# Decoding float64 weights on three engines: sign bits written by GpSimd as 16 bits, rescales on ScalarE, first high-part casts on ScalarE

## The chip, the cores and the metric

The kernel runs on one core of a Trainium2 chip. The metric is the device time of one execution in microseconds (us), and lower is better. Times are medians of several executions; one further execution was recorded by the hardware profiler, and all rows below come from it. Engines are named as the profile names them: PE is TensorE (PEld its weight loads), DVE is VectorE, ACT is ScalarE, POOL is GpSimd, SP is the queue that issues most DMAs.

## The reference

Attention with a local window and a few global keys, followed by a feed-forward layer whose activation is a rational function:

```python
scores = scale * np.matmul(q, k.transpose(0, 1, 3, 2))        # 4 batches, 8 heads, 768 x 64
keep = is_global | is_local                                   # 8 global keys, window of 96
bias = -slopes[:, None, None] * dist[None, :, :]
scores = np.where(keep, scores + bias, -1e9)
a = softmax(scores)                                           # 1e-9 added to the sum
x = np.matmul(a, v)                                           # then (3072 tokens, 512)
h = x @ w_in                                                  # 512 x 2048
P = a0 + a1*h + a2*h**2 + a3*h**3
Q = 1.0 + abs(b0)*abs(h) + abs(b1)*h**2
out = ((P / (Q + 1e-6)) @ w_out).astype(np.float32)           # 2048 x 512
```

`w_in` and `w_out` are float64 arrays. [...]

## The kernel before

**Work and order.** Tokens go in 12 chunks of 256. A chunk has 8 attention units (`u`, a pair of heads for 128 tokens) and 8 feed-forward steps (`f`, 256 of the 2048 hidden columns). The feed-forward runs some 10 to 12 units behind the attention. Each piece of work is given a priority (`PRI`, `PRI_A`), and a list scheduler turns priorities and its own estimates of durations into one fixed order per engine; at run time each engine takes its instructions strictly in that order, waiting on semaphores. So moving one operation to another engine can reorder all engines nearby.

**Weights.** Both matrices are cut into 32 pieces of 128 x 512 values, 512 KB each as float64. `first` and `WSCHED` set the order of the pieces: they are numbered 0 to 31 as they are decoded, and `MODE[n]` says how piece `n` is decoded. `fetch` (L182) issues the DMA into one of six raw buffers (three of a pool "raw", three of a pool shared with later tiles `g`). A raw buffer is free for the next fetch when the last decode operation has read it. In a raw buffer the low and the high word of each value lie side by side, so an operation on one of them steps by 8 bytes.

`decode` builds the value in two parts that are joined bit by bit:
- the scaled high word: on ACT as an absolute value (L213; mode 2), or on POOL with its sign, which the later shift throws out (L211; mode 5);
- the three bits that the shift would lose, from the upper half of the low word, on POOL (L215), written as an integer over the low word;
- the sign bit, put beside those three bits on DVE (L218);
- shift by three and join, on DVE (L220). Its output is the float32 piece, `w_..f`.

**Split.** From the second chunk on, the feed-forward uses each weight as a high part in a reduced float32 format plus a remainder, three matmuls per product. `split_w` makes the high part by a cast (L233, on DVE for the pieces in `HI_V`, otherwise ACT) and the remainder by a subtraction (L234, on DVE for the pieces in `LO_V`, otherwise POOL). The first chunk uses the undivided float32 pieces (L274, L353).

**Names.** `r_2_3` is the raw buffer of piece (1, 2, 3), that is row block 2, column block 3 of `w_in`; `r_9` that of row block 9 of `w_out`; `w_..f` the decoded, `w_..h` the high part. The profile leaves the last number of a name out. `tk`, `s`, `tp` and `o` are the attention's PSUM tiles, which share three buffers; `kF` and `qz` hold transposed keys and queries (L413, L415; POOL copies eight global keys into `kF`, L451); L463 masks the scores and takes their maximum on DVE and so frees `s`. `h`, `fu`, `fa`, `fs` and `q` belong to the activation: ACT reads `h` (L306 to L308), DVE builds the numerator (L313, L314) and the quotient (L327 to L329), POOL adds the denominator (L315), and `acc` collects the output of the second matmul.

Of the kernel before, what the change touches and what calls it, by code (L numbers as in the profile page):

```python
# [11 lines left out]
I32 = mybir.dt.int32  # L12
BF16 = mybir.dt.bfloat16
U16 = mybir.dt.uint16
AF = mybir.ActivationFunctionType
ALU = mybir.AluOpType
PSUM = bass.MemoryType.PSUM
# [22 lines left out]

SPLITS = {4: 0, 5: 2, 6: 4, 7: 8, 8: 12, 9: 16, 10: 19, 11: 22, 12: 25, 13: 28, 14: 32}

MODE = (5, 2, 2, 5, 2, 5, 2, 5, 2, 5, 2, 5, 2, 2, 5, 2, 2, 5, 2, 2, 5, 2, 2, 2, 2, 2, 2, 2, 2, 2, 2, 2)
HI_V = (0, 2, 4, 6, 8, 10, 12, 14, 16, 18, 20, 22, 24, 26, 28, 30)
LO_V = (13, 15, 17, 19, 21, 23, 25, 27, 29, 31)


# [58 lines left out]
def tile_kernel(ctx: ExitStack, tc: tile.TileContext, q, k, v, n_global, n_local,  # L106
                w_in, w_out, ca, cb, out):
    nc = tc.nc
# [52 lines left out]
    def piece(dt, key):  # L161
        return wide.tile([P, 2 * TOK], dt, tag="w", name=f"w{'_'.join(map(str, key))}{'f' if dt is F32 else 'h'}",
                         bufs=NCT * DF // (2 * TOK) + NFT + 1)
# [20 lines left out]
    def decode(key):  # L184
# [3 lines left out]
        raw = fetched.pop(key)  # L188
        bits = dst.bitcast(I32)
        top, low = raw.bitcast(I32)[:, :, 1], raw.bitcast(I32)[:, :, 0]  # L190
        half = raw.bitcast(U16).rearrange("p f (w z) -> p f w z", z=2)[:, :, 0, 1]
        mode = MODE[len(full) - 1]
        if mode < 2:


            nc.scalar.activation(out=dst, in_=raw[:, :, 1], func=AF.Abs)
            guard = nc.gpsimd if mode else nc.vector
            guard.tensor_scalar(out=dst, in0=dst, scalar1=1.125 * 2.0 ** -15, scalar2=None, op0=ALU.max)
            nc.vector.tensor_scalar(out=bits, in0=bits, scalar1=3, scalar2=0x3FFFFFFF,
                                    op0=ALU.logical_shift_left, op1=ALU.bitwise_and)  # L200
            nc.vector.scalar_tensor_tensor(out=bits, in0=top, scalar=-0x40000000, in1=bits,
                                           op0=ALU.bitwise_and, op1=ALU.bitwise_or)
            nc.vector.scalar_tensor_tensor(out=bits, in0=low, scalar=29, in1=bits,
                                           op0=ALU.logical_shift_right, op1=ALU.bitwise_or)
# [7 lines left out]
        else:  # L212
            nc.scalar.activation(out=dst, in_=raw[:, :, 1], func=AF.Abs, scale=2.0 ** -112)  # L213
        if mode != 3:
            nc.gpsimd.tensor_scalar(out=low, in0=half, scalar1=2.0 ** -13, scalar2=FLOOR, op0=ALU.mult, op1=ALU.add)  # L215
        else:
            nc.scalar.activation(out=low, in_=half, func=AF.Copy, scale=2.0 ** -13, bias=FLOOR)
        nc.vector.scalar_tensor_tensor(out=low, in0=top, scalar=-0x80000000, in1=low,  # L218
                                       op0=ALU.bitwise_and, op1=ALU.bitwise_or)
        nc.vector.scalar_tensor_tensor(out=bits, in0=bits, scalar=3, in1=low,  # L220
                                       op0=ALU.logical_shift_left, op1=ALU.bitwise_or)

# [8 lines left out]
    def split_w(key):  # L231
        hi[key] = piece(FR, key)
        (nc.vector.tensor_copy if len(hi) - 1 in HI_V else nc.scalar.copy)(out=hi[key], in_=full[key])  # L233
        (nc.vector if len(hi) - 1 in LO_V else nc.gpsimd).tensor_tensor(  # L234
# [14 lines left out]
    def load_coef():  # L249
# [6 lines left out]
        m, y, z, k = (rt[:, x:x + 1] for x in range(4))  # L256
        nc.scalar.activation(out=m, in_=coef[:, 5:6], func=AF.Abs)
        nc.vector.tensor_scalar(out=y, in0=m, scalar1=1e-36, scalar2=None, op0=ALU.max)
        nc.scalar.activation(out=y, in_=y, func=AF.Ln)
        nc.scalar.activation(out=y, in_=y, func=AF.Exp, scale=0.5)  # L260
        nc.vector.reciprocal(out=z, in_=y)
# [298 lines left out]
    def windowed(lates):  # L560
# [37 lines left out]
        for t in range(NU + LAG + F2 + 1):  # L598
# [76 lines left out]
            for n, (kind, j) in enumerate(WSCHED.get(t, ())):  # L675
                tc.cur_priority = base + 1000 * t + pri[False]["dec"] + 50 * n
                for key in pieces(kind, j):
                    decode(key)
# [162 lines left out]
```

## Time and profile before

| | |
|---|---|
| median of 3 runs | 761.07 us (759.77 to 762.39) |
| the profiled execution | 761.35 us |
| its span, first to last instruction | 759.6 us |
| mean granted TensorE clock | 0.991 |
| PE busy | 733.3 us (97%), 5074 matmuls |
| DVE busy | 607.3 us (80%) |
| ACT busy | 578.1 us (76%) |
| POOL busy | 454.8 us (60%) |
| HBM read, written | 35.92 MB, 6.29 MB |

The profiled execution's time is 1.75 us more than its span. The busy shares are means over the whole run. The decoding lies in the first 91 us, in which the weights are also read; the split follows up to 159 us; after that no work on weights is left.

### The profile page before, as it was taken

How to read it: one execution, taken by the hardware profiler on the slowest of the kernel's cores; microseconds unless marked ns; L12 is line 12 of the kernel's file. 1: busy time of each engine (PE TensorE's matmuls, PEld its weight loads, DVE VectorE, ACT ScalarE, POOL GpSimd, SP SyncE). 2: the span in 40 equal slices, each digit the busy share in tenths (PEclk: the TensorE clock that was granted, in tenths of full speed). 3: DMA queues.
4: the chain of work that ended last, by engine and by line, in shares of the span. 5: the costliest groups of instructions: out<-in, count | busy, mean ns of one | idle time of the engine just before them, and what ended most of it. 6: DMA issues, size and time to landing. Idle time of an engine off the chain costs nothing.

```text
span 759.6 us, 15075 instructions
## 1 busy us (share of the span) xinstructions
PE 733.3 (97%) x5074; PEld 637.2 (84%) x5074; DVE 607.3 (80%) x1441; ACT 578.1 (76%) x1301; POOL 454.8 (60%) x490
## 2 busy tenths in 40 slices
PE   5798899999999999999999999999999999999996
PEld 4575566888989999999999989988989988998994
DVE  6899966877798878888788878878888788876564
ACT  5788667976987877877877877877887878876764
POOL 6786564674566765756665656566467566655441
PEclk9999899999999999999999999999999999999998
DMA  8887100114333322323322322233322321200000
GB/s 255 290 272 240 41 22 22 50 25 108 95 78 74 100 62 64 98 62 73 101 54 57 105 60 63 86 76 77 95 53 64 95 68 37 71 16 1 28 1 33
DMA packets 111675, 62.16 MB, mean 82 GB/s; under 512 B 81380, under 2 KB 99812, under 8 KB 111588
## 3 DMA queue, kind: packets, MB, share of 16 engines
q1 hardware_dynamic: 110528, 60.85, 29.5%
q8 instruction: 42, 0.69, 0.4%
q10 hardware_dynamic: 1060, 0.26, 0.2%
q14 instruction: 45, 0.37, 0.2%
HBM read 35.92 MB, written 6.29 MB: 56 GB/s over the span
## 4 chain that ended last, share of the span: by engine, by line
PE 88%; DVE 7%; issue 2%; ACT 1%; DMA 1%; POOL 0%; SPq 0%; DVEq 0%; ACTq 0%
PE h L282 34%; PE acc L358 33%; PE o L524 5%; PE tp L499 5%; PE s L449 5%; PE acc L353 3%; DVE r L218 2%; PE tk L394 1%; PE h L274 1%; PE s L444 1%; DMA r<-in_moe_w_in_dram 1%; DVE pr L463 1%; ACT pr L473 0%; PE o L515 0%; DVE w_3f L220 0%
## 5 line engine op out<-in xcount | busy, mean ns | idle before, releaser
L489 POOL TENSOR_SCALAR pr<-pr,stats 128x256 f32<-128x256 f32 (+1 forms) x152 | 132.0, 879 | 112.3 <-DVE stats L480 65.0
L282 PE MATMUL h<-xh,win_l 128*128 128x256 f32 x704 | 197.4, 281 | 0.0
L315 POOL TENSOR_TENSOR fa<-fa,fs 128x512 f32<-128x512 f32 x95 | 122.9, 1293 | 86.6 <-ACT fs L308 79.6
L358 PE MATMUL acc<-wout_l,g 128*128 128x512 f32 x352 | 139.4, 396 | 0.0
L282 PEld LDWEIGHTS h<-xh,win_l 128*128 128x128 f32 x704 | 133.1, 189 | 1.6 <-issue 0.2
L338 POOL TENSOR_TENSOR g<-fu,g 128x512 fp32r<-128x512 f32 x87 | 113.2, 1301 | 32.6 <-ACT g L337 26.4
L473 ACT ACTIVATE pr<-pr,stats 128x256 f32<-128x256 f32 (+1 forms) x192 | 92.7, 485 | 30.8 <-DVE stats L463 29.9
L306 ACT ACTIVATE fu<-h,coef 128x512 f32<-128x512 f32 (+1 forms) x97 | 75.0, 774 | 30.4 <-PE h L282 24.1
L327 DVE SCALAR_TENSOR_TENSOR fu<-fu,coef,q 128x512 f32<-128x512 f32 (+1 forms) x97 | 71.8, 740 | 27.4 <-ACT q L323 24.1
L322 ACT ACTIVATE fs<-fa,coef 128x512 f32<-128x512 f32 (+1 forms) x97 | 69.5, 716 | 26.0 <-POOL fa L315 24.3
L313 DVE TENSOR_TENSOR fu<-fu,h 128x512 f32<-128x512 f32 (+1 forms) x97 | 65.6, 676 | 20.4 <-ACT fs L308 20.3
L358 PEld LDWEIGHTS acc<-wout_l,g 128*128 128x128 f32 x352 | 66.4, 189 | 9.5
L314 DVE SCALAR_TENSOR_TENSOR fu<-fu,coef,h 128x512 f32<-128x512 f32 (+1 forms) x97 | 71.7, 739 | 1.9
L427 DVE SCALAR_TENSOR_TENSOR kq<-tk,kq 64x256 fp32r<-64x256 f32 x144 | 60.8, 423 | 15.0 <-ACT kq L426 10.7
L501 DVE COPY pT<-tp 128x512 f32<-128x512 f32 (+1 forms) x75 | 48.5, 646 | 30.1 <-PE tp L499 29.0
L328 DVE SCALAR_TENSOR_TENSOR q<-fa,coef,q 128x512 f32<-128x512 f32 (+1 forms) x97 | 72.1, 744 | 0.0
L426 ACT ACTIVATE kq<-tk 64x256 fp32r<-64x256 f32 x144 | 54.2, 376 | 19.7 <-DVE kq L427 12.5
L329 DVE SCALAR_TENSOR_TENSOR fu<-q,fu 128x512 f32<-128x512 f32 (+1 forms) x97 | 66.2, 683 | 1.6
L308 ACT ACTIVATE fs<-h,coef 128x512 f32<-128x512 f32 (+1 forms) x97 | 66.3, 683 | 1.4 <-DMA out_dram<-o 1.2
L337 ACT CAST g<-fu 128x512 fp32r<-128x512 f32 (+1 forms) x89 | 54.8, 615 | 14.7 <-DVE fu L329 14.3
L307 ACT ACTIVATE fa<-h,coef 128x512 f32<-128x512 f32 (+1 forms) x97 | 65.5, 676 | 0.1
L499 PE MATMUL tp<-ident,pr 128*128 128x128 f32 x352 | 58.3, 279 | 4.9 <-ACT kF L415 3.2
(256 smaller groups left out, 2055.8 us busy)
## 6 DMA issues: line engine op xcount, KB each, us to landing
mv<-nat SPq DMA_DIRECT2D x36, 256.0 KB
qT<-kq SPq DMA_DIRECT2D x144, 64.0 KB
r<-in_moe_w_in_dram SPq DMA_DIRECT2D x16, 512.0 KB
r<-in_moe_w_out_dram SPq DMA_DIRECT2D x16, 512.0 KB
nat<-in_q_dram SPq DMA_DIRECT2D x48, 128.0 KB
vt<-in_v_dram SPq DMA_DIRECT2D x48, 128.0 KB
out_dram<-o SPq DMA_DIRECT2D x24, 256.0 KB
nat<-in_k_dram SPq DMA_DIRECT2D x46, 128.0 KB
```

Of the source, the lines that this page charges most:

```text
L282: nc.tensor.matmul(out=hps[f][:, y, :], lhsT=w[:, fs], rhs=x[:, ct, :], start=(n == 0), stop=(n == 3 * NCT - 1))
L306: nc.scalar.activation(out=u, in_=h, func=AF.Identity, scale=a3, bias=a2)
L314: nc.vector.scalar_tensor_tensor(out=u, in0=u, scalar=a1, in1=h, op0=ALU.add, op1=ALU.mult)
L315: side(f).tensor_tensor(out=a, in0=a, in1=s, op=ALU.add)
L322: nc.scalar.activation(out=s, in_=a, func=AF.Ln, bias=q1)
L327: nc.vector.scalar_tensor_tensor(out=u, in0=u, scalar=a0, in1=r, op0=ALU.add, op1=ALU.mult)
L328: nc.vector.scalar_tensor_tensor(out=r, in0=a, scalar=q1, in1=r, op0=ALU.add, op1=ALU.mult)
L338: side(f).tensor_tensor(out=g[:, 1, ys], in0=u, in1=g[:, 0, ys], op=ALU.subtract)
L358: nc.tensor.matmul(out=acc, lhsT=gs[f][:, z, y, ts], rhs=w, start=(ft == 0 and n == 0), stop=(ft == NFT - 1 and n == 2))
L473: nc.scalar.activation(out=d, in_=d, func=AF.Exp, scale=-1.0, bias=st[:, x:x + 1], accum_out=st[:, 2 + 2 * x:3 + 2 * x])
L489: nc.gpsimd.tensor_scalar(out=d, in0=d, scalar1=st[:, 6 + x:7 + x], scalar2=None, op0=ALU.mult)
L499: nc.tensor.transpose(out=t_ps[:, x, w, :], in_=pr[:, x, w, :], identity=ident)
```

## The change

`MODE` gets a new value, 6, for the 14 odd pieces from 3 to 29. In mode 6 ACT makes the scaled absolute value, POOL makes the three bits as before, and POOL then writes the sign as a 16-bit integer, 0 or -32768, into the upper half of the word that holds the three bits. DVE's L218 is left out for these pieces and only the shift and join remains. Eight of the nine pieces that were in mode 5 leave it (six for mode 6, two for mode 2); piece 0 keeps it. `HI_V` changes too: the casts of pieces 0, 2, 4, 6, 8 and of all later even ones go to ACT, and those of the odd pieces from 9 to 31 go to DVE.

```diff
+I16 = mybir.dt.int16
...
-MODE = (5, 2, 2, 5, 2, 5, 2, 5, 2, 5, 2, 5, 2, 2, 5, 2, 2, 5, 2, 2, 5, 2, 2, 2, 2, 2, 2, 2, 2, 2, 2, 2)
-HI_V = (0, 2, 4, 6, 8, 10, 12, 14, 16, 18, 20, 22, 24, 26, 28, 30)
+MODE = (5, 2, 2, 6, 2, 6, 2, 6, 2, 6, 2, 6, 2, 6, 2, 6, 2, 6, 2, 6, 2, 6, 2, 6, 2, 6, 2, 6, 2, 6, 2, 2)
+HI_V = (9, 11, 13, 15, 17, 19, 21, 23, 25, 27, 29, 31)
 LO_V = (13, 15, 17, 19, 21, 23, 25, 27, 29, 31)
...
-        nc.vector.scalar_tensor_tensor(out=low, in0=top, scalar=-0x80000000, in1=low,
-                                       op0=ALU.bitwise_and, op1=ALU.bitwise_or)
+        if mode == 6:
+            sign = raw.bitcast(I16).rearrange("p f (w z) -> p f w z", z=2)[:, :, 0, 1]
+            nc.gpsimd.tensor_scalar(out=sign, in0=raw[:, :, 1], scalar1=0.0, scalar2=-32768.0,
+                                    op0=ALU.is_lt, op1=ALU.mult)
+        else:
+            nc.vector.scalar_tensor_tensor(out=low, in0=top, scalar=-0x80000000, in1=low,
+                                           op0=ALU.bitwise_and, op1=ALU.bitwise_or)
         nc.vector.scalar_tensor_tensor(out=bits, in0=bits, scalar=3, in1=low,
                                        op0=ALU.logical_shift_left, op1=ALU.bitwise_or)
```

In the changed kernel the lines above the new branch stand one further down (L213 is L214, L215 is L216), the sign is L221, the old L218 is L224, the old L220 is L226, and everything below stands six further down.

What each engine is given, in order, differs up to the third chunk and is the same after it. Three places follow. First POOL, at the pieces 19 to 28, before; the numbers behind a name tell one buffer use from another:

```order
L211 TENSOR_SCALAR w_8f<-r_8_761 128x512
L215 TENSOR_SCALAR r_8_761<-r_8_761 128x512
L215 TENSOR_SCALAR r_9_768<-r_9_768 128x512
L215 TENSOR_SCALAR r_0_3_775<-r_0_3_775 128x512
L451 COPY kF<-kGF 128x8
L215 TENSOR_SCALAR r_1_3_782<-r_1_3_782 128x512
L215 TENSOR_SCALAR r_2_3_860<-r_2_3_860 128x512
L215 TENSOR_SCALAR r_3_3_867<-r_3_3_867 128x512
L315 TENSOR_TENSOR fa_736<-fa_736,fs_737 128x512
L215 TENSOR_SCALAR r_10_931<-r_10_931 128x512
```

POOL now, from the same three bits of piece 22 on:

```order
L216 TENSOR_SCALAR r_0_3_775<-r_0_3_775 128x512
L216 TENSOR_SCALAR r_1_3_782<-r_1_3_782 128x512
L221 TENSOR_SCALAR r_9_768<-r_9_768 128x512
L457 COPY kF<-kGF 128x8
L216 TENSOR_SCALAR r_2_3_860<-r_2_3_860 128x512
L221 TENSOR_SCALAR r_1_3_782<-r_1_3_782 128x512
L216 TENSOR_SCALAR r_10_931<-r_10_931 128x512
L216 TENSOR_SCALAR r_3_3_867<-r_3_3_867 128x512
L321 TENSOR_TENSOR fa_736<-fa_736,fs_737 128x512
L216 TENSOR_SCALAR r_12_1016<-r_12_1016 128x512
L221 TENSOR_SCALAR r_3_3_867<-r_3_3_867 128x512
```

A sign stands three or four places behind the three bits of its piece, and a kF copy or a sum for the activation can stand behind a sign. Second DVE, between two groups of L463, before:

```order
L218 SCALAR_TENSOR_TENSOR r_11_938<-r_11_938 128x512
L314 SCALAR_TENSOR_TENSOR fu_735<-fu_735,coef,h_717 128x512
L218 SCALAR_TENSOR_TENSOR r_12_1016<-r_12_1016 128x512
L552 TENSOR_TENSOR o_840<-o_840,rs_854 128x256
L220 SCALAR_TENSOR_TENSOR w_10f<-w_10f,r_10_931 128x512
L233 CAST w_2_0h<-w_2_0f 128x512
L218 SCALAR_TENSOR_TENSOR r_13_1023<-r_13_1023 128x512
L220 SCALAR_TENSOR_TENSOR w_11f<-w_11f,r_11_938 128x512
L327 SCALAR_TENSOR_TENSOR fu_735<-fu_735,coef,q_810 128x512
L328 SCALAR_TENSOR_TENSOR q_810<-fa_736,coef,q_810 128x512
L313 TENSOR_TENSOR fu_817<-fu_817,h_799 128x512
L220 SCALAR_TENSOR_TENSOR w_12f<-w_12f,r_12_1016 128x512
```

DVE now, between the same two groups:

```order
L226 SCALAR_TENSOR_TENSOR w_10f<-w_10f,r_10_931 128x512
L224 SCALAR_TENSOR_TENSOR r_12_1016<-r_12_1016 128x512
L226 SCALAR_TENSOR_TENSOR w_12f<-w_12f,r_12_1016 128x512
L484 TENSOR_REDUCE stats<-stats 128x2
L486 RECIPROCAL stats<-stats 128x2
L333 SCALAR_TENSOR_TENSOR fu_735<-fu_735,coef,q_810 128x512
L334 SCALAR_TENSOR_TENSOR q_810<-fa_736,coef,q_810 128x512
L558 TENSOR_TENSOR o_840<-o_840,rs_854 128x256
L226 SCALAR_TENSOR_TENSOR w_3_3f<-w_3_3f,r_3_3_867 128x512
L335 SCALAR_TENSOR_TENSOR fu_735<-q_810,fu_735 128x512
L224 SCALAR_TENSOR_TENSOR r_14_1093<-r_14_1093 128x512
L319 TENSOR_TENSOR fu_817<-fu_817,h_799 128x512
```

The sign operations of the odd pieces and the cast are gone, and `fu_735` is finished ahead of the second group. Third PE, from the transposes `tp_921` on, before:

```order
L499 MATMUL tp_921<-ident,pr_792 128x128 x4
L353 MATMUL acc_0_747<-w_2f,fu_647 128x512
L353 MATMUL acc_0_747<-w_3f,fu_647 128x512
L353 MATMUL acc_1_757<-w_2f,fu_647 128x512
L353 MATMUL acc_1_757<-w_3f,fu_647 128x512
L444 MATMUL s_944<-kF,qz 128x256 x2
L400 MATMUL tk_960<-ident,nat_557 128x128 x2
L274 MATMUL h_889<-x_277,w_0_2f 128x256
```

PE now, up to the same transposes:

```order
L359 MATMUL acc_1_757<-w_2f,fu_647 128x512
L359 MATMUL acc_1_757<-w_3f,fu_647 128x512
L280 MATMUL h_889<-x_277,w_0_2f 128x256
L280 MATMUL h_889<-x_277,w_1_2f 128x256
L280 MATMUL h_889<-x_277,w_2_2f 128x256
L280 MATMUL h_889<-x_277,w_3_2f 128x256
L280 MATMUL h_889<-x_277,w_0_2f 128x256
L505 MATMUL tp_921<-ident,pr_792 128x128 x4
```

Feed-forward matmuls have moved ahead of the transposes: four `acc` (the other two stand a few rows up) and five `h`. In the same way the four `acc` of `w_4f` and `w_5f` and the eight `h_955` behind them now stand ahead of `o_996`.

## The prediction

> **What bounds the kernel now.** I read the page's slices first, then stretches, the chain, PE's waits and single instructions. The slices hold busy tenths:
>
> ```profile
> PE   5798899999999999999999999999999999999996
> ...
> DVE  6899966877798878888788878878888788876564
> ...
> PEclk9999899999999999999999999999999999999998
> ```
>
> A slice is 19 us. TensorE is full from the sixth slice on, so whatever is gained or lost is decided in the first 100 us. The stretches confirm that (columns: from and to, length, us busy and instructions of PE, PEld, DVE, ACT and POOL, granted clock, DMA share, GB/s):
>
> ```profile
> 10.00:45.00 35.00, 26.68 (x171) 19.62 (x170) 29.73 (x90) 25.70 (x89) 27.27 (x29) 0.95 0.93 293
> 45.00:70.00 25.00, 24.45 (x143) 18.64 (x143) 24.93 (x52) 21.64 (x51) 18.36 (x19) 1.00 0.75 231
> 70.00:100.00 30.00, 25.25 (x106) 16.03 (x102) 29.07 (x58) 21.14 (x49) 18.64 (x19) 0.89 0.27 85
> 100.00:700.00 600.00, 600.00 (x4330) 533.22 (x4329) 485.20 (x1160) 470.40 (x1040) 366.78 (x393) 1.00 0.26 67
> ```
>
> From 100 to 700 us PE has no idle time: a start made earlier by a microsecond ends a microsecond earlier. From 45 to 100 us PE idles 0.55 + 4.75 = 5.3 us, while DVE has 54.0 of 55 us filled, ACT 42.8 and POOL 37.0. The chain that ended last, asked for 9 to 86 us alone, names the engine:
>
> ```profile
> by line: DVE r L218 23.9%; issue 15.4%; DMA r<-in_moe_w_in_dram 8.4%; DVE pr L463 7.0%; ACT pr L473 4.1%; DVE w_3f L220 3.7%; DVE fu L313 3.2%; DVE w_2f L220 3.1%; DVE q L328 2.8%; DVE w_0f L220 2.8%; PE s L444 2.7%; POOL r L215 2.3%; POOL
> ```
>
> L218, the operation that mode 6 drops, has 23.9% of 77 us = 18.4 us of that chain, 0.58 us for each of its 32. What DVE's lateness costs PE is two gaps, and a lower clock behind each (waits of PE; then its instructions in time: start, us):
>
> ```profile
> PE tp L499 <- ACT kF L415: 2.6, 1, 2.6
> PE o L515 <- DVE stats L463: 2.5, 2, 2.1
> ```
> ```profile
> 72.95 1.12 PE L499 MATMUL tp<-ident,pr 128*128 128x128 f32 x4 [2.62 <-ACT kF L415]
> 73.86 1.92 PE L353 MATMUL acc<-w_2f,fu 128*128 128x512 f32 x2
> 75.56 1.44 PE L353 MATMUL acc<-w_3f,fu 128*128 128x512 f32 x2
> 76.84 1.02 PE L353 MATMUL acc<-w_2f,fu 128*128 128x512 f32 x2
> ...
> 83.09 0.60 PE L499 MATMUL tp<-ident,pr 128*128 128x128 f32 x4
> 85.75 0.44 PE L515 MATMUL o<-ident,stats 128*64 128x128 f32 x4 [2.06 <-DVE stats L463]
> ...
> 88.22 1.11 PE L499 MATMUL tp<-ident,pr 128*128 128x128 f32 x4
> 89.13 1.48 PE L353 MATMUL acc<-w_4f,fu 128*128 128x512 f32 x2
> ```
>
> Idle: 2.62 + 2.06 = 4.7 us. After the first gap the same work takes 1.12, 1.92 and 1.44 us instead of 0.60, 1.02 and 1.02 (1.8 us lost), after the second 1.11 and 1.48 instead of 0.60 and 1.02 (1.0 us). Together 7.5 us that a less loaded DVE could give back in this stretch.
>
> **The change part by part.** Prices (mean ns stand behind the busy time; of L211 and L215 minimum/median/maximum):
>
> ```profile
> L218 DVE SCALAR_TENSOR_TENSOR r<-r 128x512 int32<-128x512 int32 x32 | 25.9, 816 | 1.8 <-POOL r L215 1.8
> L215 POOL TENSOR_SCALAR r<-r x32: 641/860/1647, 11.0 to 80.3; 128x512 int32<-128x512 uint16 x32
> L211 POOL TENSOR_SCALAR w_0f<-r x2: 1523/1684/1845, 9.4 to 14.2; 128x512 f32<-128x512 f32 x2
> sum 91.00, POOL 15.63; mean POOL 7.82
> L213 ACT ACTIVATE w_3f<-r 128x512 f32<-128x512 f32 x4 | 2.7, 684 | 0.0
> L233 ACT CAST w_1h<-w_1f 128x512 fp32r<-128x512 f32 x3 | 1.9, 617 | 0.2
> L233 DVE CAST w_0h<-w_0f 128x512 fp32r<-128x512 f32 x2 | 1.3, 645 | 0.0
> L233 DVE CAST w_1h<-w_1f 128x512 fp32r<-128x512 f32 x2 | 0.8, 414 | 0.0
> ```
>
> - (a) Fourteen L218 go from DVE: 14 x 0.82 = 11.4 us of work, on the chain 14 x 0.58 = 8.1 us.
> - (b) Casts: high parts 0, 2, 4, 6, 8 leave DVE, 9 and up in odd numbers replace 10 and up in even ones. Before 100 us DVE loses four (1.3 + 0.8 = 2.1 us) and ACT gains four (4 x 0.62 = 2.5 us). Later DVE makes twelve where it made twelve, with nobody waiting on PE.
> - (c) Eight pieces leave mode 5. GpSimd loses eight of its nine L211 (15.63 / 9 = 1.74 us each, 13.9 us); ScalarE gains eight rescales at 0.68 us, 5.5 us; six of them fall before 45 us.
> - (d) GpSimd gains fourteen sign writes, an operation that the trace does not have: float32 in, a compare and a multiply, 16 bits out, both with gaps of 8 bytes. Nearest rows: L215, two ALU operations and 16 bits on one side, at least 0.64 us; L211, the same float32 input, 1.52 us. I take 1.54 us, by the input. Fourteen cost 21.6 us (9.0 at 0.64), so GpSimd's balance is +7.7 us (-4.9 at the low end). The high end is open: if each ALU operation costs what L211's one does, 3.1 us and 43 us.
>
> GpSimd's cover from 45 to 100 us: 37.0 us filled, less two L211 (3.5), plus eight signs, of pieces 15 to 29 (12.3) = 45.8 of 55 us. It holds, and would be used up at a sign of (55 - 33.5) / 8 = 2.7 us. Behind each sign in its queue wait the kF copies for the scores and the fa sums of the feed-forward, by one sign at most; the decode of an odd piece waits for it on DVE, where the order puts it behind the next even piece.
>
> ACT from 45 to 100 us: 42.8 + 2.5 (casts) + 1.4 (two rescales) = 46.7 of 55 us. Its cover is 12.2 us of idle time, part of it waiting for DVE or PE; I put 1.5 of the added 3.9 us on the path.
>
> The order takes up DVE's relief: tp_921, the first gap, now stands behind four acc and five h matmuls, and o_996, the second, behind acc of w_4f and w_5f. Those need DVE's fu earlier than before, which (a) allows. The transfers follow, since a raw buffer is freed by DVE's last operation on it:
>
> ```profile
> SPq L182 <- DVE w_3f L220: 4.7, 3, 2.8
> ACT w_10f L213 <- DMA r<-in_moe_w_out_dram: 1.1, 1, 1.1
> ```
>
> In odd pieces that release now waits for GpSimd's sign, and on SP the next q and k loads wait behind it. In the changed order they still stand between the weights, several units ahead of their use; I put this at nothing, with 2.8 us (the longest such wait) as its upper end.
>
> Before 45 us the first h waits for the attention of chunk 0:
>
> ```profile
> 44.85 1.03 PE L274 MATMUL h<-x,w_0f 128*128 128x256 f32 x4
> ```
>
> DVE's chain gets shorter by 6 x 0.58 = 3.5 us, ACT busier by 6 x 0.68 = 4.1 us on 25.7 of 35, DMA is 0.93 busy: I take nothing, with -3.5 and +4.1 as ends.
>
> Sum: -7.5 (gaps and clock) + 1.5 (ACT) = -6.0 us. The profiled execution took 761.35 us (span 759.6), 0.28 us above the median of 761.07: 755.4 us.
>
> **A rule against it.** What GpSimd does beside DVE is in the trace (GpSimd's and DVE's instructions in time):
>
> ```profile
> 35.12 1.54 POOL L211 TENSOR_SCALAR w_3f<-r 128x512 f32<-128x512 f32 x1
> 78.89 1.33 POOL L315 TENSOR_TENSOR fa<-fa,fs 128x512 f32<-128x512 f32 x1
> ```
> ```profile
> 35.21 1.72 DVE L218 SCALAR_TENSOR_TENSOR r<-r 128x512 int32<-128x512 int32 x2
> ...
> 79.01 1.76 DVE L218 SCALAR_TENSOR_TENSOR r<-r 128x512 int32<-128x512 int32 x1
> ...
> 84.33 0.68 DVE L218 SCALAR_TENSOR_TENSOR r<-r 128x512 int32<-128x512 int32 x1
> ```
>
> Beside L315, with two inputs, DVE's L218 stood still for most of its length (1.76 us, against 0.68 with GpSimd idle). Beside L211, with one, two L218 took 1.72 us together, some 0.4 us more than twice 0.68. So a one-input sign should hold DVE up by about 0.4 us, not by its 1.54.
>
> The Trainium skill, "SBUF — State Buffer", section "Who interferes with whom", says otherwise: VectorE with two SBUF inputs and a GpSimd operation that reads SBUF exclude each other for the whole instruction. The L315 row agrees, the L211 row does not. By that rule rival 1 below would be the outcome.
>
> **Rivals.**
> 1. *The relief is taken back by the shared access or by ACT: no change.* Were exclusion complete, signs would cost the pair 14 x 1.54 = 21.6 us against 13.9 + 14 x 0.68 = 23.4 us given back: 1.8 us over the whole start, 1 us or so in the end, 760.5. ACT alone could do it too, by 5.5 + 2.5 = 8.0 us of new work. The L211 row speaks against the first, ACT's idle time against the second. 25%.
> 2. *GpSimd becomes the bound: slower.* From a sign of 2.7 us on. At 3.1 us it has 33.5 + 8 x 3.1 = 58.3 us to do in 55, +3.3 us, and before that 27.3 - 6 x 1.74 + 6 x 3.1 = 35.5 in 35, +0.5 us: 765.2. For it: a float32 tensor_scalar costs 1.52 us with one ALU operation. Against: L215 has two at 0.64 us. 20%.
> 3. *All of the chain comes back.* 8.1 + 0.9 (the cast at 78 us) = 9.0 us, with a sign near L215's price and an earlier first h: 752.4. 10%.
>
> **How the numbers follow.** The forecast (755.4, own range 753 to 759) has 45%. About 0.3%, 2.3 us, is what a measurement of this kernel can tell from no change (its three runs lay 2.6 us apart): below 758.8 faster, above 763.4 slower. Faster: 0.44 of the forecast's 0.45 and rival 3, 0.54. Same: rival 1 and what is left, 0.27. Slower: 0.19. The range goes from rival 3 to beyond rival 1, to where the start's +4.1 or the q and k loads' +2.8 take part of the forecast's gain and more: 752 to 764. It leaves out most of rival 2.
>
> **What would show it.** Right: signs of 0.6 to 1.9 us; L218 at 18; PE's two gaps gone and the clock near 1.00 from 70 to 100 us; DVE with idle time there; a first h within 3 us of 45. Wrong: signs over 2.7 us, GpSimd full to 90 us with kF and fa late; PE waiting for ACT casts or rescales; or DVE's two-input operations stretched by a sign's length.

## The result, and the profile after

| | before | after |
|---|---|---|
| median of 5 runs | 759.77 us (758.76 to 762.39) | 765.40 us (764.38 to 765.43) |
| ratio of the means, 95% interval | | 1.0064 [1.0044, 1.0085] |
| span of the profiled execution | 759.6 us | 763.6 us |

The change makes the kernel 0.64% slower, some 5 us. 755.4 us were predicted, and 765.4 lies above the range too. The sign's own row, and the row of the three bits behind which it stands (minimum/median/maximum, first and last start):

```profile
L221 POOL TENSOR_SCALAR r<-r x14: 2692/3042/3213, 15.2 to 95.3; 128x512 int16<-128x512 f32 x14
L216 POOL TENSOR_SCALAR r<-r x32: 639/1088/1195, 11.0 to 99.2; 128x512 int32<-128x512 uint16 x32
```

A sign costs 2.69 us where none of DVE's decode or activation operations runs beside it, and 3.04 in the median: twice the 1.54 us that the sum took, and above the 2.7 us at which GpSimd's cover was to end. The page's slices show where it goes:

```profile
PE   5698889999999999999999999999999999999996
...
DVE  6658786879788888888788778788888788886565
...
POOL 6999986575567666656556657565466656665441
PEclk9999999999999999999999999999999999999998
```

DVE's full slices have gone, and POOL has taken their place from the second to the fifth. The stretches:

```profile
10.00:45.00 35.00, 26.32 (x148) 18.94 (x147) 24.42 (x77) 26.79 (x87) 32.81 (x26) 0.95 0.93 286
45.00:70.00 25.00, 22.73 (x133) 17.59 (x133) 17.18 (x45) 19.06 (x47) 23.75 (x19) 1.00 0.66 197
70.00:100.00 30.00, 25.98 (x131) 16.25 (x130) 23.59 (x45) 20.37 (x50) 28.88 (x20) 1.00 0.41 123
```

POOL fills 52.6 of the 55 us from 45 to 100 (before: 37.0), DVE 40.8 (before: 54.0), and PE idles 2.27 + 4.02 = 6.3 us (before: 5.3). DVE and ACT now wait for POOL, and PE for DVE behind them (waits of DVE and of ACT from 9 to 105 us, of PE from 45 to 105 us):

```profile
DVE r L224 <- POOL r L216: 10.8, 13, 1.9
DVE w_5f L226 <- POOL r L221: 2.8, 1, 2.8
```
```profile
ACT fs L328 <- POOL fa L321: 8.7, 4, 4.9
```
```profile
PE acc L359 <- DVE fu L335: 3.2, 2, 2.4
```

One place in time, on POOL, ACT, DVE and PE:

```profile
74.86 3.20 POOL L221 TENSOR_SCALAR r<-r 128x512 int16<-128x512 f32 x1
78.14 2.42 POOL L216 TENSOR_SCALAR r<-r 128x512 int32<-128x512 uint16 x2
80.64 1.81 POOL L321 TENSOR_TENSOR fa<-fa,fs 128x512 f32<-128x512 f32 x1
```
```profile
82.48 0.72 ACT L328 ACTIVATE fs<-fa,coef 128x512 f32<-128x512 f32 x1 [2.28 <-POOL fa L321]
```
```profile
87.69 0.68 DVE L335 SCALAR_TENSOR_TENSOR fu<-q,fu 128x512 f32<-128x512 f32 x1
```
```profile
88.42 1.12 PE L359 MATMUL acc<-w_4f,fu 128*128 128x512 f32 x2 [2.43 <-DVE fu L335]
```

The last input of this `fa` sum was written at 72.74 us (ACT's L314, 72.03 and 0.71 long). The sum starts at 80.64, because the sign of 3.20 us and the three bits of other pieces stand before it in POOL's order. ACT stands still for it; DVE, which has the L224 of a piece ahead of the rest of `fu` in its order, stands still for 1.90 us until 83.23 for the three bits behind the sum; and PE gets its longest gap between 45 and 105 us.

Not every gap is the sign's. The longest before 45 us is 2.29 us, ahead of the scores matmuls at 37.31, and the profile puts it down to POOL's L216. But ACT's copy into `kF`, which they read, ends only at 37.21, and in run 5, where the sign is short, the same matmuls start at 37.47. The eight h matmuls behind them, before and after:

```profile
37.59 1.89 PE L274 MATMUL h<-x,w_0f 128*128 128x256 f32 x8
```
```profile
40.32 2.85 PE L280 MATMUL h<-x,w_0f 128*128 128x256 f32 x8
```

The clock is 1.00 from 37.5 to 39.5 us before and 0.65 from 40.0 to 43.2 in the change. Run 5 has these eight at 39.54 us with 2.65 us, so most of this delay does not come from the length of the sign.

A mark that both kernels pass is the first matmul with split weights, before and after:

```profile
115.08 0.68 PE L282 MATMUL h<-xh,w_0h 128*128 128x256 f32 x1
```
```profile
119.08 0.47 PE L288 MATMUL h<-xh,w_0h 128*128 128x256 f32 x1
```

It is 4.0 us late, and so is the end (763.6 against 759.6). In both, 486 matmuls stand before the mark, and from it to the end it is 644.5 us: all was lost before it. I use it below; a mark comes from one execution, and runs 13 and 14, which turned out as two of the same, have it 1.8 us apart.

### The profile page after: what moved, and what is told of

Read it like the earlier page. It is cut to its first block, busy times and chain, and to the rows that moved or that the text cites. A ratio compares the mean times of both kernels' runs of the same rounds, so it can differ in the third digit from the quotient of the medians.

```text
span 763.6 us, 15062 instructions
## 1 busy us (share of the span) xinstructions
PE 734.6 (96%) x5074; PEld 636.7 (83%) x5074; DVE 596.5 (78%) x1423; ACT 582.9 (76%) x1313; POOL 484.2 (63%) x496
## 4 chain that ended last, share of the span: by engine, by line
PE 87%; POOL 4%; DMA 3%; DVE 2%; issue 2%; ACT 1%; SPq 0%; POOLq 0%; DVEq 0%
PE h L288 33%; PE acc L364 32%; PE o L530 5%; PE tp L505 5%; PE s L455 4%; PE acc L359 2%; POOL r L216 2%; PE tk L400 1%; PE h L280 1%; PE s L450 1%; POOL r L221 1%; DMA r<-in_moe_w_in_dram 1%; DMA vt<-in_v_dram 1%; POOL win_l L240 1%; DMA r<-in_moe_w_out_dram 0%
## 5 line engine op out<-in xcount | busy, mean ns | idle before, releaser
L321 POOL TENSOR_TENSOR fa<-fa,fs 128x512 f32<-128x512 f32 x95 | 124.5, 1311 | 86.5 <-ACT fs L314 81.9
L479 ACT ACTIVATE pr<-pr,stats 128x256 f32<-128x256 f32 (+1 forms) x192 | 92.7, 485 | 27.9 <-DVE stats L469 27.0
L314 ACT ACTIVATE fs<-h,coef 128x512 f32<-128x512 f32 (+1 forms) x97 | 66.3, 683 | 1.2 <-DMA out_dram<-o 0.7
```

The source lines that it names most:

```text
L321: side(f).tensor_tensor(out=a, in0=a, in1=s, op=ALU.add)
L479: nc.scalar.activation(out=d, in_=d, func=AF.Exp, scale=-1.0, bias=st[:, x:x + 1], accum_out=st[:, 2 + 2 * x:3 + 2 * x])
```

## The experiments

G is the theory that what the sign occupies makes the kernel slow (S in the first texts: its time on GpSimd alone). Against it stand A, ScalarE's added work, and O, the order that the list scheduler makes. All ratios are to the kernel before, on the same chip, with 95% intervals. In every kernel made from the changed one the sign keeps its line, L221, but for the two tables of prices.

**1. The sign from 16 bits.**

```diff
-in0=raw[:, :, 1]                    # float32
+in0=words[:, :, 1, 1]               # its upper 16 bits as int16
```

> The sign operation reads the upper 16 bits of the high word as int16 instead of the whole word as float32; the same two ALU operations, the same int16 output, the same function, and every engine has the same instructions in the same order as in the changed kernel. Three theories. S (the price of the sign operation fills GpSimd): the price comes from the float32 input, as in L212's 1.52 us for one ALU operation; with 16-bit input the sign costs 0.64 to 1.2 us as L216 does with two ALU operations, 14 of them give back 20 to 28 us of GpSimd between 15 and 95 us, and the time falls to 753 to 757 us (ratio to before 0.993 to 0.998). A (ScalarE's added rescales and casts make it slower): the time stays within 1 us of the changed kernel's 765. O (the new order of the plan makes it slower): the order is unchanged, so the time stays at 765 too. If the compare or the int16 output sets the price, the sign stays at 2.7 us and the time at 765, which would say nothing between S, A and O.

764.71 us, ratio 1.0052 [1.0036, 1.0068].

```profile
L221 POOL TENSOR_SCALAR r<-r x14: 2678/3048/3215, 14.3 to 93.0; 128x512 int16<-128x512 int16 x14
```

The price is the same with half the input. The reason that the prediction gave for its 1.54 us, the input's type, is wrong, and between G, A and O the run tells nothing.

**2. A table of prices** (the sign replaced by seven forms in turn, two of each).

> The sign of the 14 pieces is replaced by seven kinds of operation in turn (most of these weights get wrong sign bits; the time is not read, only the mean of each kind): 0 float32 in, compare alone, int16 out; 1 float32 in, multiply and add, int16 out; 2 int16 in, compare and multiply, int16 out; 3 float32 in, compare and multiply, float32 out; 4 int16 in, compare alone; 5 float32 in, multiply alone, int16 out; 6 as in the changed kernel. If a float32 input pays per ALU operation (L212: one, 1.52 us; L221: two, 2.69 us): kinds 0 and 5 at 1.5, kinds 1, 3 and 6 at 2.7, kinds 2 and 4 near 0.65. If the compare is what costs: kind 1 near 1.5, kind 2 near 2.7. If the int16 output is what costs: kind 3 near 1.5 and kinds 2 and 4 high.

Five of the forms, kinds 1 to 5:

```profile
L226 POOL TENSOR_SCALAR r<-r x2: 1662/1686/1711, 14.5 to 52.0; 128x512 int16<-128x512 f32 x2
L228 POOL TENSOR_SCALAR r<-r x2: 2698/2867/3036, 18.1 to 55.0; 128x512 int16<-128x512 int16 x2
L230 POOL TENSOR_SCALAR r<-r x2: 1994/2153/2312, 25.4 to 64.4; 128x512 f32<-128x512 f32 x2
L232 POOL TENSOR_SCALAR r<-r x2: 2258/2270/2283, 30.7 to 69.1; 128x512 int16<-128x512 int16 x2
L234 POOL TENSOR_SCALAR r<-r x2: 2750/2754/2759, 35.4 to 73.4; 128x512 int16<-128x512 f32 x2
```

None of the three readings holds. The second has its two numbers nearly right (multiply with add 1.69, compare with multiply on 16 bits 2.87), but a multiplication without any compare takes 2.75. Multiply with add (the first row) is the cheapest; the forms with a compare (second to fourth) are dear, and so is one multiplication (the last); with 32 bits out (the third) the pair costs 0.7 us less than with 16. Run 8 goes on from here.

**3. The casts divided as before, the signs kept** (`HI_V` of the kernel before).

> The changed kernel with the casts of the high parts divided between ScalarE and VectorE as before; the signs stay on GpSimd. S: GpSimd is as full as with the whole change, so 763 to 766 us; VectorE, which was busy 24 of 30 us at 70 to 100 us, takes the 2 us of casts beside its waits. A: ScalarE is relieved of 2.5 us before 100 us, and the time falls by 1 to 3 us to 762 to 764 us. O: the order of 1540 rows of VectorE and 2790 of TensorE changes, so the time may move by some us in either direction.

770.13 us, 1.0122 [1.0095, 1.0148]: slower by another 0.6%. S and A expected no such thing; O had allowed for it. The profiled execution shows where: the mark is at 119.87 us, 0.8 later than in the change, and from there to the end it is 648.0 us instead of 644.5, with the same matmuls left to do and no sign among them. So most of the loss lies in the new order behind the mark and not in the casts beside the decoding.

**4. The casts alone** (`MODE` of the kernel before, `HI_V` of the change).

> Only the second part of the change: the casts of the first 9 high parts on ScalarE, and all pieces decoded as before the change. S: the decode by GpSimd is as before, VectorE is relieved of 2.1 us of the chain until 86 us, so 758 to 760 us against 759.8 before (ratio 0.997 to 1.001). A: the casts on ScalarE cost 1 to 2.5 us, so 761 to 762 us. O: the order differs little from the one before the change, so within 1 us of before.

759.73 us, 0.9983 [0.9968, 0.9997]; the mark is at 112.55 us in its profiled execution. The casts help a little, and the interval ends just short of no help.

**5. The sign on 16 columns of 512.**

```diff
-out=sign, in0=raw[:, :, 1]
+out=sign[:, :16], in0=raw[:, :16, 1]
```

> The sign operation covers 16 of the 512 columns only (the other columns of the 14 pieces keep no sign, so their weights are wrong); it has the same place on GpSimd, the same reads of VectorE behind it, and the plan differs from the changed kernel's by 339 lines of TensorE's 21536 and 408 of VectorE's. S (the price of the sign fills GpSimd): 14 x 2.9 = 41 us leave GpSimd, which then has 20 to 25 us to do in 45 to 100 us, and the time falls below before: 752 to 757 us, ratio 0.990 to 0.997. A (ScalarE's added rescales and casts): they are all still there, so the time stays within 1.5 us of the changed kernel, ratio 1.004 to 1.008. O (the plan): most of the new order is still there, so the ratio stays above 1.002.

754.19 us, 0.9902 [0.9879, 0.9924].

```profile
L221 POOL TENSOR_SCALAR r<-r x14: 294/612/1410, 15.6 to 74.1; 128x16 int16<-128x16 f32 x14
```
```profile
45.00:70.00 25.00, 24.12 (x134) 18.22 (x133) 22.56 (x53) 24.21 (x60) 17.11 (x25) 1.00 0.74 237
70.00:100.00 30.00, 29.10 (x144) 19.06 (x143) 27.55 (x55) 25.13 (x58) 21.08 (x20) 1.00 0.26 78
```

With all of ScalarE's new work in place, PE idles 1.8 us from 45 to 100 us instead of 6.3, and the kernel is 7 us faster than before. A falls as the cause, and the forecast's mechanism stands: the change gains where the sign is nearly free. How much of this gain is VectorE's 14 operations, and how much the eight rescales that GpSimd loses and the casts, was not taken apart. Run 17 excludes the data as the reason.

**6. Seven signs instead of 14** (`MODE` 6 for the pieces 3, 7, 11, ... 27 and 2 for the others).

> Seven pieces instead of 14 have the sign on GpSimd (every fourth piece from the fourth on); the other seven go to VectorE with two operations, and ScalarE rescales all of them as in the changed kernel, so ScalarE's added work is unchanged. S: half of the signs leave GpSimd (20 us), which then has 10 to 12 us to spare in 45 to 100 us, and VectorE gets back 7 L224 of 0.67 us alone (4.7 us) where it has 13 us to spare: 755 to 760 us, ratio 0.995 to 1.000. A: unchanged, ratio 1.004 to 1.008. O: the plan differs from the changed kernel's by 404 lines of VectorE and 356 of TensorE, so the ratio stays near 1.005.

764.62 us, 1.0045 [1.0026, 1.0063]. S expected 755 to 760, so the time does not follow the number of signs alone (the order differs too). Here VectorE is full again (27.9 of 30 us from 70 to 100), and PE waits for it:

```profile
88.26 1.11 PE L505 MATMUL tp<-ident,pr 128*128 128x128 f32 x4 [4.45 <-DVE stats L469]
```

**7. No signs on GpSimd** (`MODE` 2 for all pieces but the first, `HI_V` of the change).

> No sign on GpSimd at all: all 31 pieces after the first are rescaled by ScalarE and decoded by two VectorE operations, and the casts are those of the change, so the ScalarE work added by the change is there in full and GpSimd has 8 rescales fewer than before. S: VectorE is the bound again as before the change, less the 2.1 us of casts: 757 to 761 us, ratio 0.996 to 1.001. A: ScalarE's 8 us of new work cost 3 to 5 us: 763 to 765 us, ratio 1.004 to 1.007. O: the order is another again (2790 lines of TensorE), so anything in between.

763.99 us, 1.0031 [1.0018, 1.0044]: above S's range and just below A's. Against run 4 it differs by the eight rescales that go from GpSimd to ScalarE, and by its order. These together cost about 0.5%, part of it behind the mark (646.5 us to the end, against 644.6 in run 4). Run 5 has the same work on ScalarE and is the fastest kernel of all, so it is no price that adds up; that it is paid where VectorE is the bound as well is an argument, not shown.

**8. The second table of prices.**

> Seven kinds of operation in the place of the 14 signs in turn (some of them are no sign; the time is not read, only the mean of each kind): 0 float32 in, multiply by 0 and add -0, bfloat16 out (which leaves only the sign bit); 1 the same with the upper half of the word as bfloat16 in; 2 int16 in, multiply and add, int16 out; 3 float32 in, multiply alone, bfloat16 out; 4 float32 in, multiply and add, float32 out; 5 float32 in, compare and multiply, bfloat16 out; 6 int16 in, multiply and add, float32 out. The first table of kinds had multiply with add at 1.66 us from float32 to int16 and L216 at 0.65 from uint16 to 32 bits, against 2.26 to 2.75 for each kind with a compare or with one operation. P (multiply followed by add is a cheap pair of its own): kinds 0, 1, 2, 4 and 6 at 0.6 to 1.7 us, 3 and 5 at 2.0 to 2.8. R (16 bits out are what is dear, 32 bits out are cheap): kinds 4 and 6 at 0.6 to 1.6, all others at 1.6 to 2.8.

In the order of the kinds 0 to 6, and the single multiplication that the kernel has anyway:

```profile
L225 POOL TENSOR_SCALAR r<-r x2: 1665/1732/1800, 43.6 to 77.7; 128x512 bf16<-128x512 f32 x2
L227 POOL TENSOR_SCALAR r<-r x2: 1347/1522/1697, 15.2 to 48.1; 128x512 bf16<-128x512 bf16 x2
L229 POOL TENSOR_SCALAR r<-r x2: 1691/1738/1785, 18.8 to 56.2; 128x512 int16<-128x512 int16 x2
L231 POOL TENSOR_SCALAR r<-r x2: 2247/2507/2767, 26.5 to 61.5; 128x512 bf16<-128x512 f32 x2
L233 POOL TENSOR_SCALAR r<-r x2: 672/890/1109, 32.1 to 66.2; 128x512 f32<-128x512 f32 x2
L235 POOL TENSOR_SCALAR r<-r x2: 3018/3030/3043, 34.4 to 69.4; 128x512 bf16<-128x512 f32 x2
L237 POOL TENSOR_SCALAR r<-r x2: 659/660/661, 40.7 to 77.0; 128x512 f32<-128x512 int16 x2
L212 POOL TENSOR_SCALAR w_0f<-r x1: 1520/1520/1520, 9.4 to 9.4; 128x512 f32<-128x512 f32 x1
```

Both P and R hold in part, and the price is made of two terms that add up. Multiply with add costs 0.66 us to 32 bits, whatever the input; a single multiplication 0.86 us more (1.52), compare with multiply 1.33 us more (1.99, run 2). And 16 bits out cost 0.7 us on top where no decode or activation operation of DVE runs beside (1.34 in run 9 instead of 0.66, 2.25 instead of 1.52, 2.69 in the change instead of 1.99); the larger extras, up to 1.2 us (2.75, 3.02), stand only in rows with such an operation beside them. The sign of the change has both extras: 0.66 + 1.33 + 0.7 = 2.69. Kinds 0 and 1 leave the same sign bit at 1.67 and 1.35 us; both of kind 0's rows stood beside DVE's work, and run 10 shows 1.34 for it too.

**9 and 10. The same bit at the price that the prediction took.**

```diff
-    scalar1=0.0, scalar2=-32768.0, op0=ALU.is_lt, op1=ALU.mult     # float32 to int16
+    scalar1=0.0, scalar2=-0.0, op0=ALU.mult, op1=ALU.add           # 9: bfloat16 to bfloat16; 10: float32 to bfloat16
```

> The sign is written by another pair of operations that leaves the same bit: the upper half of the high word, read as bfloat16, times 0 plus -0, written as bfloat16, which is +0 or -0 and so the sign bit alone. This pair took 1.35 us alone and 1.70 beside VectorE's two-input operations. Everything else is as in the change, but the order changes with it (2692 lines of TensorE's 21536). S: GpSimd gets back 14 x 1.3 = 19 us, its sign is at the price that the prediction took (1.54 us), and the prediction's sum should come out: -4 to -7 us against before, ratio 0.991 to 0.995. A: ScalarE's added work is unchanged, ratio 1.002 or more. O: the plan is another one, so anything from 0.990 to 1.010; a result near 0.993 speaks against O only together with the run that follows.

> As the run before with every instruction in the same order on every engine; the only difference is that the sign reads the whole high word as float32, which took 1.67 us alone instead of 1.35. S: 14 x 0.33 = 4.6 us more of GpSimd's time, still under the 2.7 us at which its cover ends: at most 2 us slower than the run before, ratio to before 0.991 to 0.997. A and O: no difference from the run before beyond 0.5 us.

9: 765.55 us, 1.0065 [1.0048, 1.0083]. 10: 765.24 us, 1.0063 [1.0046, 1.0080]. S misses: the signs take 22.0 us of GpSimd instead of 41.7, and in the end nothing is gained over the change. A's number would fit, but run 5 has the same work on ScalarE at 0.990. Run 10 comes out as run 9, and its signs last as long (1.34 us at least, 1.66 in the median). The mark of run 9 is at 117.09 us, 2.0 later than before; the other half of its loss, 1.9 us, lies behind the mark (646.4 us to the end), as in run 3. The sign's row, and the stretch from 70 to 85 us, of run 9:

```profile
L221 POOL TENSOR_SCALAR r<-r x14: 1336/1664/1872, 14.7 to 74.4; 128x512 bf16<-128x512 bf16 x14
```
```profile
70.00:85.00 15.00, 10.98 (x49) 5.77 (x48) 15.00 (x29) 12.16 (x30) 12.19 (x12) 0.89 0.53 159
```

GpSimd is no longer the bound; VectorE is, with 15.00 of 15 us. It does not do more operations, each takes longer. Total of L224 and L226 (the two operations of the decode on DVE) from 9 to 105 us, DVE's column alone, first of the change, then of the narrow sign, then of run 9:

```profile
9.00:105.00 96.00, 12.73 (x18) 0.98 0.66 199
9.00:105.00 96.00, 28.89 (x32) 0.98 0.66 199
```
```profile
9.00:105.00 96.00, 14.01 (x18) 0.98 0.63 200
9.00:105.00 96.00, 27.31 (x32) 0.98 0.63 200
```
```profile
9.00:105.00 96.00, 18.16 (x18) 0.98 0.64 198
9.00:105.00 96.00, 32.38 (x32) 0.98 0.64 198
```

The same 50 operations take 41.6 us beside the dear sign, 41.3 beside the narrow one and 50.5 beside the cheap one: 9.2 us more than with the narrow sign, 0.66 us for each of the 14. These sums hold what all of GpSimd's instructions do to DVE. Counted row by row, the operations of L224 and L226 that overlap a sign exceed 0.68 us each by 2.6 us together in the change, by 1.4 beside the narrow sign and by 8.5 in run 9; the rest lies mostly beside L216. One place (POOL's sign, then DVE, of run 9):

```profile
62.19 1.87 POOL L221 TENSOR_SCALAR r<-r 128x512 bf16<-128x512 bf16 x1
```
```profile
62.17 0.68 DVE L226 SCALAR_TENSOR_TENSOR w_8f<-w_8f,r 128x512 int32<-128x512 int32 x1
62.77 1.56 DVE L226 SCALAR_TENSOR_TENSOR w_9f<-w_9f,r 128x512 int32<-128x512 int32 x1
```

The first operation passes beside the sign, the second is held up by 0.9 us, and the sign itself by 0.5. The sign had 1.29 us to run when the second began, so DVE did not stand still for all of it. In the change an L226 of 0.68 us lies unharmed inside a sign of 3.20:

```profile
63.39 3.20 POOL L221 TENSOR_SCALAR r<-r 128x512 int16<-128x512 f32 x1
```
```profile
64.62 0.68 DVE L226 SCALAR_TENSOR_TENSOR w_8f<-w_8f,r 128x512 int32<-128x512 int32 x1
```

Others are held up a little (0.96 us at 84.03, inside the sign that starts at 83.28). So the dear form mostly leaves DVE alone and fills GpSimd; the cheap form spares GpSimd and takes DVE's time. From here on G means both costs.

**11. The cheap sign with the casts of before; 12. the cheap sign on seven pieces.**

> The cheap sign of the first of these runs with the casts of the high parts divided as before the change, so that the casts' part is seen once without a full GpSimd. S: VectorE, which then has some 10 us to spare, takes the 2 us of casts: within 1.5 us of the first of these runs. A: ScalarE is relieved of 2.5 us, 1 to 2 us faster than the first. O: the order changes again, so up to 5 us in either direction, as the old casts with the dear sign did (+5 us).

> The cheap sign on seven pieces; VectorE decodes the other seven in two operations; ScalarE rescales all. S with VectorE as the second bound: VectorE has 7 L224 more (4.7 us), GpSimd 7 signs fewer (10 us); since VectorE was the engine that delayed TensorE in the seven-piece run with the dear sign (ratio 1.0045), this one loses against the first of these runs: ratio 0.996 to 1.002. A: equal to the first. O: anything.

11: 768.58 us, 1.0102 [1.0083, 1.0121], slower than run 9 by 0.4%, where S and A expected nothing or a gain. Twice now the old casts have cost more with signs on GpSimd than run 4's 0.17%; here too nearly all of it lies behind the mark (117.51 us, then 649.7). 12: 765.88 us, 1.0067 [1.0049, 1.0086], as run 9, as A had it and above what S expected; fewer signs again do not help, though 3.6 us of its loss lie behind the mark (648.1).

**13 and 14. One order, and the whole word written.**

```diff
-out=sign, ... scalar1=0.0, scalar2=-32768.0, op0=ALU.is_lt, op1=ALU.mult
+out=raw[:, :, 0], ... scalar1=0.0, scalar2=-0.0, op0=ALU.mult, op1=ALU.add     # 13
+out=raw[:, :, 0], ... scalar1=0.0, scalar2=1.0, op0=ALU.mult, op1=ALU.mult     # 14
```

> The sign operation of the 14 pieces is multiply by 0 and add -0 with the whole word written as float32 (it overwrites the three bits, so these weights lose their last three bits); this form took 0.67 us alone. All 512 columns are read and written. The order is near that of the narrow sign (112 lines of TensorE differ) and far from that of the 1.35 us sign (2545 lines). G (GpSimd's occupation by the sign, in itself and in VectorE's stretched operations): near the narrow sign's 0.990: 0.989 to 0.994. O (the list scheduler's order decides, not the price): the same, as the order is near. The run sets the low end of a dose whose order is fixed.

> Every engine has the same instructions in the same order as in the run before; the sign's second operation is a multiplication by 1 instead of an addition of -0 (again the three bits are overwritten). Compare with multiply took 2.0 us to 32 bits, so I expect 1.5 to 2.0 us instead of 0.67. G: 14 x 1.1 = 15 us more on GpSimd and VectorE held up with it: 2 to 6 us slower than the run before. O: the order is the same, so no difference beyond 0.5 us. If the pair of multiplications turns out to cost 0.67 too, the run tells nothing but that.

13: 761.69 us, 1.0017 [0.9999, 1.0035]. 14: 762.13 us, 1.0015 [0.9999, 1.0031]. The pair of multiplications turned out as cheap as the other (median 0.99 against 0.97 us), so 14 is a repetition of 13 and tells that only. 13 misses its range: at 0.97 us a sign, in an order near that of the narrow one, all of the narrow sign's gain is lost again.

```profile
L221 POOL TENSOR_SCALAR r<-r x14: 657/969/1138, 15.2 to 76.7; 128x512 f32<-128x512 f32 x14
```
```profile
9.00:105.00 96.00, 14.26 (x18) 0.98 0.63 198
9.00:105.00 96.00, 32.03 (x32) 0.98 0.63 198
```
```profile
PE acc L359 <- DVE fu L335: 3.3, 2, 1.8
```

L224 and L226 take 46.3 us, 5.0 more than beside the narrow sign, and PE waits for DVE's `fu` (waits from 45 to 105 us). The mark stands at 115.38 us, with the narrow sign at 110.80; behind it the two take 644.6 and 644.2 us.

**15 and 16. A 1.35 us sign and a 2.25 us sign in orders near the narrow one's** (15: run 9's sign for the odd pieces 3 to 31; 16: run 9's with the multiplication alone).

> The sign at 1.35 us (bfloat16 in and out, the same bit) on 15 odd pieces from 3 to 31 instead of 14 from 3 to 29. The order that the list scheduler makes of it is near that of the narrow sign (157 lines of TensorE) and far from that with 14 pieces (2448 lines), which took 1.0065 with the same price. G: one sign more cannot help; at the same price the ratio stays at 1.004 to 1.008. O: as the narrow sign's order, 0.990 to 0.995 plus the price of the signs, at most 0.998.

> The sign as one multiplication by 0 from bfloat16 to bfloat16, which leaves the same bit; one multiplication took 2.25 us with bfloat16 out. Its order is again near the narrow sign's (134 lines of TensorE). G: 14 x 2.25 us leave GpSimd between the 1.35 us sign and the 2.7 us one, both of which took 1.0065: the same. O: as the narrow sign's order plus the price, 0.992 to 1.000, so clearly faster than the 1.35 us sign in the other order.

15: 763.99 us, 1.0037 [1.0023, 1.0051]. 16: 762.33 us, 1.0023 [1.0009, 1.0038]. Run 15 has run 9's price and is about 2 us faster in another order, with one sign more. The mark says where: run 15 has it at 118.32 us, later than run 9, and takes 644.3 us from there instead of 646.4. So the order is worth about 2 us, behind the mark, and at the mark the cheap sign is 2.0 (run 9) and 3.2 us (run 15) worse than before. O, which had it below 0.998, misses; G's range begins just above. L224 and L226 take 16.4 + 33.1 = 49.5 us in run 15, about as in run 9 (49 operations instead of 50). In 16 the dearer sign holds DVE up less (16.4 + 29.6 = 45.9 us) and fills GpSimd more; its time misses both texts, under the 1.0065 of G and over the 1.000 of O. Set beside run 13 it tells more: the sums of L224 and L226 are alike (45.9 and 46.3 us), the signs take 35.2 us of GpSimd instead of 12.7, and the two kernels are equally fast. There 22.5 us more on GpSimd cost nothing that can be seen. That fits the prediction's cover of GpSimd, which was to end at a sign of 2.7 us: in the mean it is 2.51 here (GpSimd fills 51.3 of the 55 us from 45 to 100) and 2.98 in the change.

**17. The change with nearly the narrow sign's data** (the compare against -3e38, so no sign is set).

> The changed kernel with the compare against -3e38 instead of 0: the same instructions in the same order and of the same kind, but the 14 pieces get no sign, so the data in the feed-forward are nearly those of the narrow sign's run. If the values of the data are what made that run fast, this one comes near its ratio of 0.990. If they are not (G), it stays at the changed kernel's 1.004 to 1.008, and the narrow sign's 0.990 is due to what the full sign occupies.

766.38 us, 1.0060 [1.0040, 1.0079], as the change itself. The data are not the reason for run 5.

**18. No sign, and the cheap pair for the rescale.**

```diff
-scalar1=2.0 ** -112, scalar2=None, op0=ALU.mult)
+scalar1=2.0 ** -112, scalar2=0.0, op0=ALU.mult, op1=ALU.add)
```

> A version from the findings, with no sign on GpSimd: the casts alone (ratio 0.9983), and the rescale of 8 pieces on GpSimd written as multiply and add 0, a pair that took 0.67 us where the single multiplication takes 1.52 (piece 9 goes to ScalarE, which keeps the order near that of the casts alone, 115 lines of TensorE). If a shorter operation of GpSimd is also a shorter hold-up of VectorE: 0.9 us less on each of 8, of which VectorE sees 0.1 to 0.2 us each, 1 to 2 us: ratio 0.994 to 0.998. If the fast pair holds VectorE up as long as the slow operation did: no gain beyond the casts alone, 0.997 to 1.000.

760.26 us, 0.9988 [0.9975, 1.0002]. The rescale falls from 1.52 to 0.65 us at least, GpSimd's busy time from 10 to 70 us from 45.6 to 38.0 us (with one such piece fewer), and nothing is gained over run 4. VectorE stays full (55.5 of these 60 us), and L224 and L226 take 54.3 us as against 54.0: the shorter rescale did not hold it up less, in sum. Run 4 remains the best kernel that computes the whole function, 0.17% ahead of before.

## Why the prediction was wrong, point by point

- **(d) The sign's price: the term that was mis-sized.** 1.54 us was taken "by the input", with 3.1 as the upper end; at least 2.69 and 2.98 in the mean were measured (14 took 41.7 us). That is the step which failed. Neither the input (run 1) nor the count of ALU operations (0.66 us for two of them, run 8) sets the price, but the kind of the pair and the 16 bits out. The nearest row was no guide here: L215 is cheap for being multiply with add to 32 bits.
- **Rival 2, GpSimd becomes the bound,** is what happened, at its mechanism, its place and nearly its number: 765.2 worked out for 3.1 us, 765.4 measured. It had 20%. What it foretold is in the rows: GpSimd full to 100 us, `fa` late (8.7 us of ACT's waits), L224 behind L216. That the numbers meet is in part luck: it worked out 3.8 us over before, and the ratio says 4.9, the profiles 4.0.
- **The hold-up of VectorE: seen and not summed.** "Some 0.4 us" for each sign was read off the L211 row, used against the rule, and then left out of the sum; 14 of it are 5.6 us, nearly the whole forecast of -6.0. Run 9 shows what that omission alone does: at the predicted price 9.2 us together by the sums, 8.5 by the rows beside signs, and a mark 2.0 us later than before instead of earlier. Run 15, at the same price in another order, has its mark 3.2 us later. Had the sign cost 1.54 us, the forecast would have been wrong all the same.
- **Rival 1, shared access,** is thus half right. On the Trainium skill's rule ("SBUF — State Buffer", "Who interferes with whom") the rows stand between (the page calls the shared ports an exclusive lock; "for the whole instruction" it writes of VectorE's two-port modes): beside the dear sign DVE's operation of two inputs ran in its usual 0.68 us, against the rule; beside the cheap one the next was held up by 0.9 of the 1.29 us that the sign still ran, nearer to it. Which forms hold DVE up was measured here for these few only.
- **(a) VectorE's relief** was right in its mechanism, and its size is not contradicted: L224 is at 18, and with a sign that occupies little the whole change gains 7 us (run 5), against 6.0 to 9.0 in the forecast and in rival 3.
- **(b) The casts** helped by 0.17% alone (run 4). **(c) The rescales on ScalarE** were put at 1.5 us with the casts. Run 5 carries them all and shows no such cost; run 7 shows 0.5% against run 4, with VectorE full and another order.
- **PE's two gaps and the clock.** The clock is 1.00 from 70 to 100 us, as foretold. The idle time has not gone: 4.02 us there, most of it behind DVE's `fu`, whose inputs come by way of the `fa` sums that GpSimd now makes late.
- **The first h.** The row quoted at 44.85 us was not the first: eight matmuls of h stand at 37.59 us in the trace of before. Against that the change is 2.7 us late (40.32), where "within 3 us of 45" had been called right; the narrow sign is 2.0 us late there (39.54), and so is faster only by what follows.
- **The order.** From the mark to the end 14 of the 20 kernels here take 644.0 to 644.7 us; runs 3, 7, 9, 10, 11 and 12 take 646.2 to 649.7. In five of these six the same 486 matmuls stand before the mark (492 in run 7). For runs 3, 7 and 9 the texts above give 2692 to 2790 changed lines of TensorE's order. So such orders cost 1.7 to 5.2 us where no weight is decoded any more. What makes that stretch longer, with PE idle for 1.1 us at most, is open. The change and the narrow sign are not among the six, so what separates these two lies before the mark.
- **Still open.** Run 13 loses the whole gain to 5.0 us of hold-up and 4.8 us of GpSimd (12.7 us of signs against 7.9), while run 16 adds 22.5 us of GpSimd to that and loses no more; how the two combine was not taken apart. That GpSimd's own instructions beside DVE can be avoided by another place in the order wasn't tried.

## What to carry to other kernels

An operation that moves to another engine has two prices, its own time there and what it takes from the engine it was to relieve: read both off rows in which the two run side by side, and put both in the sum. A price for an operation that the trace does not show should not come from a row that is like it in one respect; the forms of one instruction went from 0.66 to 3.02 us here, and a range that wide belongs in the sum until the form itself is measured. And when a relief depends on a price, work out the price at which it ends and ask how far the unknown is from it.

## What was not expected of the hardware

On GpSimd, 128 x 512 elements with tensor_scalar take 0.66 us as multiply with add or with a second multiplication to 32 bits, but 1.52 as one multiplication and 1.99 as compare with multiply; 16 bits out cost 0.7 us more in each (1.34, 2.25 and 2.69). A second operation that changes nothing (add 0) makes the rescale 0.87 us shorter (1.52 to 0.65). How long a sign holds VectorE up does not go by its own length: by the rows that overlap a sign, L224 and L226 lost 0.41 us a sign beside the 0.66 us form, 0.61 beside that of 1.35, 0.38 beside the multiplication of 2.25, and 0.18 beside the compare of 2.69.
